# Statistics of the layer norm one tile ahead, key finals between the norms, transposes behind products, and the memory evacuated by VectorE, in a fused linear-attention and gated-MLP kernel

## The chip, the cores and the metric

The kernel runs on one core of a Trainium2 chip. The metric is the device time of one execution in microseconds (us). A run also has a state, fast or slow, told by its granted TensorE clock and its time, and only fast runs are compared. The engines are PE (TensorE, the matrix products), PEld (its weight loads, which overlap products), DVE (VectorE), ACT (ScalarE), POOL (GpSimd) and SP (SyncE, which here only issues DMA). The kernel keeps one queue of DMA on SP and one on ACT.

## The reference

With `x` of 2048 tokens by 640:

```python
xn = layernorm(x)                              # no weights
q, k, v = split(xn @ wqkv)                     # 32 heads of 20
phi = lambda t: where(t > 0, t + 1, exp(t)) + 1e-6
kv  = einsum("bhsd,bhse->bhde", phi(k), v)     # the "memory", over all tokens
o   = einsum("bhqd,bhde->bhqe", phi(q), kv) / (phi(q) . sum_s phi(k) + 1e-6)
g   = silu(relu(xn @ w1) @ w2)
out = x + (o @ wo) * g
```

## The kernel before

The tokens are 16 tiles of 128. The parts that matter here:

- **First keys.** For tiles 0 to 3 there is no time to wait for a full layer norm. The kernel subtracts the mean only (mean on ACT, `mean_act`; subtraction on DVE, `centre`), transposes the tile on PE, copies the transpose to SBUF (`xcT_copy`), multiplies by the key weights (`K_mm`), and applies the reciprocal root later, as a scale of the evacuation (`K_exp`, `K_relu` on ACT, which read `rsy`).
- **Norms.** From tile 4 on there is a true norm on DVE (`LN_norm`). Its statistics are `bn`, `bn`, `aggr` on DVE, and the reciprocal root takes two POOL instructions inside `aggr`. The normed tile is transposed by a DMA that SP issues.
- **Key finals.** `K_fin` finishes phi(k) on DVE in two instructions. Key buffers `ek` are a ring of four, so the evacuation of tile 4 may not start before the final of tile 0.
- **Up products.** `H_block` multiplies by `w1`, which arrives in three parts: 640 KB and 480 KB on SP's queue, 1040 KB on ACT's queue.
- **Memory.** `G_block` is `xn^T phi(k)`, 160 products of 320 columns, evacuated five times.

```python
    def aggr(t):
        sc.op("DVE", lambda eng: eng.bn_aggr(mv[:, t, :], stats[:, t, :, :].rearrange("p a b -> p (a b)")),
              R=[("stats", t, 0), ("stats", t, 1)], W=[("mv", t)])
        sc.op("POOL", lambda eng: eng.tensor_scalar(out=rsv[:, t:t + 1], in0=mv[:, t, 1:2], scalar1=EPS_LN,
                                                    scalar2=None, op0=ALU.add), R=[("mv", t)], W=[("rsv", t)])
        sc.op("POOL", lambda eng: eng.tensor_tensor(out=rsy[:, t:t + 1], in0=rsv[:, t:t + 1], in1=mhalf[:, :],
                                                    op=ALU.pow), R=[("rsv", t), ("mhalf",)], W=[("rsy", t)])

    def LN_stats(t):
        bn(t, 0)
        bn(t, 1)
        aggr(t)

    # ... cut ...

    def LN_norm(t):
        last_norm[0] = sc.op("DVE", lambda eng: eng.tensor_scalar(
            out=xn[:, t, :], in0=xin[:, t % XR, :], scalar1=mv[:, t, 0:1], scalar2=rsy[:, t:t + 1],
            op0=ALU.subtract, op1=ALU.mult), R=[("xin", t % XR), ("mv", t), ("rsy", t)], W=[("xn", t)])
        if t >= 4:
            xnT_dma(t)
        if t + XR < T:
            x_load(t + XR)
```

The first keys as emitted (each engine keeps the order of its own instructions in this text; waits are put in from the data):

```python
    for k in range(KA, C):
        K_mm(0, 2, k, k + 1)
        K_mm(1, 4, k, k + 1)
    bn(1, 1)
    centre(2)
    aggr(1)
    transposes(2, 0)
    mean_act(3, 0)
    bn(2, 0)
    xcT_copy(2, 0, 0, "DVE")
    xcT_copy(2, 0, 1, "DVE")
    K_exp(0, 2)
    K_mm(2, 6, 0, KA)
    K_mm(2, 6, KA, C, (0,))
    centre(3)
    transposes(3, 0)
    K_mm(2, 6, KA, C, (1,))
    bn(2, 1)
    xcT_copy(3, 0, 0, "DVE")
    xcT_copy(3, 0, 1, "ACT")
    w1_load(2, "ACT")
    K_relu(0, 2)
    aggr(2)
    K_mm(3, 0)
    K_exp(1, 4)
    K_relu(1, 4)
    LN_stats(4)
    bn(3, 0)
    bn(3, 1)
    aggr(3)
    K_exp(2, 6)
    K_relu(2, 6)
    K_exp(3, 0)
    K_relu(3, 0)
```

What goes between the up products of the first 512 tokens (`n` is the number of the up block):

```python
            if j == 0:
                if n < 4:
                    LN_norm(n + 4)
                    if n < 3:
                        LN_stats(n + 5)
                if n in (3, 4):
                    K_fin(2 * n - 6)
                    K_fin(2 * n - 5)
                if 4 <= n < 8:
                    LN_norm(n - 4)
                if 8 <= n < 12:
                    xnT_dma(n - 8)
                if n == 8:
                    w_load(wqk[:, :, 0:D], A_wqkv[:, 0:D], ("wq",), E="ACT")
```

The evacuation in `G_block`:

```python
        sc.op("ACT", lambda eng: eng.activation(out=GT[:, k, :].rearrange("p (a n) -> p a n", a=2), in_=ps2(b, HN),
                                                func=ACTF.Copy), R=[("ps", b), ("ps", b + 1)], W=[("GT", k)])
```

## Time and profile before

| | before |
|---|---|
| time, median of 3 runs | 224.86 us (224.37 to 224.89) |
| span of the profiled execution | 223.4 us |
| PE busy | 216.8 us, 97% |
| first up product starts | 12.75 us |
| keys of tile 5 start | 24.48 us |
| the 160 memory products, first start to last end | 22.15 us |

The page of the kernel before: busy time by engine, and the shares of the chain that ended last.

```profile
PE 216.8 (97%) x1442; PEld 133.8 (60%) x1442; DVE 115.0 (51%) x213; ACT 86.6 (39%) x142; POOL 45.9 (21%) x69
...
PE 83%; DVE 4%; ACTq 3%; DMA 3%; SPq 2%; ACT 1%; POOL 1%; issue 1%; DVEq 0%
```

PE is nearly always at work, so the share says little about what a change can win. The Trainium skill (Perfetto Trace Analysis, "Identifying the Most-Contended Engine") warns against TensorE's busy share as a measure of how close a kernel is to its limit. What helps is the list of holes. The timeline of PE early on (columns: start, length, engine, line, instruction, count, and in brackets the idle time just before and what ended it):

```profile
8.73 0.44 PE L470 MATMUL psT<-ident,reg 128*128 128x128 bf16 x5
9.39 1.12 PE L495 MATMUL psT<-reg,regX 128*128 128x320 bf16 x7 [0.22 <-DVE regX L480]
10.35 0.44 PE L470 MATMUL psT<-ident,reg 128*128 128x128 bf16 x5
...
11.38 1.53 PE L495 MATMUL psT<-reg,regX 128*128 128x320 bf16 x10 [0.17 <-ACT regX L482]
12.75 6.64 PE L570 MATMUL psT<-regX,reg 128*128 128x512 bf16 x30
19.22 1.52 PE L495 MATMUL psT<-reg 128*128 128x320 bf16 x10
20.58 2.32 PE L570 MATMUL psT<-regX,reg 128*128 128x512 bf16 x10
24.48 1.53 PE L495 MATMUL psT<-reg 128*128 128x320 bf16 x10 [1.58 <-ACT regE L512]
```

L470 are the transposes, L495 key products and L570 up products. Ten key products take 1.36 us from start to start, and five up products 1.08. This agrees with the Trainium skill (VectorE: DVE Perf Modes, "The TRN2 errata", TensorE row of its table): 6 plus the columns, in cycles of 2.4 GHz, is 136 ns for 320 columns and 216 ns for 512. The large hole is the 1.58 us before the keys of tile 5. The waits of the first 25 us show where it comes from (engine and line, waited for whom: total us, times, longest):

```profile
ACT regE L512 <- DVE reg L530: 3.1, 1, 3.1
DVE reg L435 <- POOL rsy L424: 3.0, 3, 1.0
...
PE psT L495 <- ACT regE L512: 1.6, 1, 1.6
```

PE waits for ACT (L512, the evacuation of tile 4), which waits 3.1 us for a key final on DVE (L530), which is behind norms (L435) that each wait 1.0 us for POOL's root.

The stretch of the memory, all engines (ACTq is ACT issuing DMA):

```profile
112.33 22.15 PE L788 MATMUL psT<-reg 128*128 128x320 bf16 x160
...
114.76 5.70 ACTq L780 DMA_DIRECT2D reg<-in_B_w_dram  x2
120.51 1.42 ACT L793 ACTIVATE reg<-psT 128x640 bf16<-128x640 f32 x2 [7.38 <-issue]
```

ACT issues weight loads until 120.46 us and only then evacuates the first memory block. 64 products of 0.1357 us after 112.33 us, at 121.02, PE would start the third block. It starts at about 121.27, 0.25 us late.

Issues of DMA (size, median us from issue to landing): the two parts of the up weights on SP's queue.

```profile
reg<-in_B_w_dram SPq DMA_DIRECT2D x1, 640.0 KB, 6.7
...
reg<-in_B_w_dram SPq DMA_DIRECT2D x1, 480.0 KB, 7.2
```

They are issued at 5.04 and 6.77 us and land at 11.7 and 14.0.

### The profile page before, as it was taken

Reading aid. Unit: us, or ns where it says so; the run is one execution under the profiler, and the core shown is the slowest. Engines: PE = TensorE matmul, PEld = TensorE weight load, DVE = VectorE, ACT = ScalarE, POOL = GpSimd, SP = SyncE. Lnnn points to the kernel's source line nnn. Section 1 sums busy time; section 2 is a strip of 40 time slices with the busy share of each in tenths; the row PEclk is TensorE's granted clock in tenths of the full one; section 3 lists DMA queues with packets and bytes.
Section 4 is the critical chain, followed back from the end, with each engine's and each line's share of the span. In section 5 each row is a group of like instructions: output and inputs, shape, how many; then the busy total and the mean of one; then the engine's idle time right before and its main releaser. Section 6 shows DMA issues by size and latency. Waiting matters only on the chain.

```text
span 223.4 us, 3512 instructions
## 1 busy us (share of the span) xinstructions
PE 216.8 (97%) x1442; PEld 133.8 (60%) x1442; DVE 115.0 (51%) x213; ACT 86.6 (39%) x142; POOL 45.9 (21%) x69
## 2 busy tenths in 40 slices
PE   8999799999999999999999999999999999999993
PEld 8655354555544555444466777677767776776672
DVE  4766996798649999783700002940424240412243
ACT  4585766656665576554412113232021102110211
POOL 2252631111041599950000005000000000000000
PEclk9999999999999999999999999999999999999999
DMA  6996389621001233000099969900010100001011
GB/s 178 283 339 130 87 248 140 190 44 29 3 1 29 59 94 115 0 0 3 11 204 321 341 245 369 323 12 3 29 59 32 59 29 32 29 29 59 3 59 60
DMA packets 27761, 23.91 MB, mean 107 GB/s; under 512 B 11873, under 2 KB 27105, under 8 KB 27745
## 3 DMA queue, kind: packets, MB, share of 16 engines
q1 hardware_dynamic: 24512, 19.50, 30.7%
q10 hardware_dynamic: 3232, 4.18, 5.4%
q8 instruction: 11, 0.18, 0.3%
q14 instruction: 6, 0.04, 0.1%
HBM read 15.81 MB, written 5.24 MB: 94 GB/s over the span
## 4 chain that ended last, share of the span: by engine, by line
PE 83%; DVE 4%; ACTq 3%; DMA 3%; SPq 2%; ACT 1%; POOL 1%; issue 1%; DVEq 0%
PE psT L840 25%; PE psT L570 21%; PE psT L548 10%; PE psT L879 9%; PE psT L495 7%; PE psT L788 6%; DMA reg<-in_A_x_dram 3%; ACTq L780 3%; DVE stats L416 2%; PE psT L817 1%; PE psT L858 1%; PE psT L587 1%; SPq L358 1%; ACTq L776 1%; POOL rsy L424 1%
## 5 line engine op out<-in xcount | busy, mean ns | idle before, releaser
L840 PE MATMUL psT<-reg,hT 128*128 128x320 bf16 x416 | 60.5, 299 | 0.0
L840 PEld LDWEIGHTS psT<-reg,hT 128*128 128x128 bf16 x416 | 40.3, 98 | 16.5 <-issue 1.1
L570 PE MATMUL psT<-reg 128*128 128x512 bf16 x195 | 46.0, 379 | 0.0
L893 DVE TENSOR_TENSOR reg<-psT,reg 128x640 bf16<-128x640 f32 (+1 forms) x17 | 13.3, 785 | 48.8 <-PE psT L879 47.6
L574 ACT ACTIVATE hT<-psT 128x512 bf16<-128x512 f32 x52 | 30.5, 601 | 17.4 <-PE psT L570 17.4
L570 PEld LDWEIGHTS psT<-reg 128*128 128x128 bf16 x195 | 18.9, 98 | 22.0 <-issue 0.4
L868 ACT ACTIVATE reg<-psT 128x640 bf16<-128x640 f32 x12 | 8.2, 702 | 43.1 <-PE psT L840 23.6
L548 PE MATMUL psT<-reg 128*128 128x512 bf16 x100 | 24.8, 379 | 0.0
L506 POOL TENSOR_TENSOR zacc<-zacc,reg 128x640 f32<-128x640 f32 x16 | 23.8, 1489 | 3.7 <-DVE reg L530 2.8
L879 PE MATMUL psT<-reg,pqT 128*128 128x320 bf16 x160 | 24.3, 299 | 0.0
L788 PE MATMUL psT<-reg 128*128 128x320 bf16 x160 | 22.1, 299 | 0.1
L512 ACT ACTIVATE regE<-psT 128x640 bf16<-128x640 f32 x24 | 15.6, 701 | 11.4 <-PE psT L495 8.3
L495 PE MATMUL psT<-reg 128*128 128x320 bf16 x120 | 18.3, 299 | 1.6 <-ACT regE L512 1.6
L788 PEld LDWEIGHTS psT<-reg 128*128 128x128 bf16 x160 | 15.6, 98 | 6.6 <-ACT reg L793 0.4
L879 PEld LDWEIGHTS psT<-reg,pqT 128*128 128x128 bf16 x160 | 15.7, 98 | 6.1
L556 DVE TENSOR_SCALAR regE<-psT 128x512 bf16<-128x512 f32 x20 | 13.6, 682 | 8.2 <-ACT regE L555 8.2
L558 DVE SCALAR_TENSOR_TENSOR pqT<-regE 128x512 bf16<-128x512 bf16 x20 | 17.4, 870 | 0.7
L548 PEld LDWEIGHTS psT<-reg 128*128 128x128 bf16 x100 | 9.8, 98 | 11.5
L495 PEld LDWEIGHTS psT<-reg 128*128 128x128 bf16 x120 | 11.7, 98 | 8.3 <-ACT regE L512 2.1
L416 DVE BATCH_NORM_STATS2 stats<-reg 128x6 f32<-128x320 bf16 x32 | 14.1, 479 | 3.3 <-DMA reg<-in_A_x_dram 3.3
L806 DVE TENSOR_TENSOR reg<-psT,mv 128x120 bf16<-128x120 f32 (+1 forms) x6 | 1.1, 261 | 27.9 <-POOL reg L910 27.9
L530 DVE TENSOR_TENSOR reg<-regE 128x640 bf16<-128x640 bf16 x16 | 14.5, 909 | 1.4 <-ACT regE L512 1.0
(68 smaller groups left out, 166.6 us busy)
## 6 DMA issues: line engine op xcount, KB each, us to landing
reg<-in_A_x_dram SPq DMA_DIRECT2D x16, 160.0 KB, 3.0
scr<-regE SPq DMA_DIRECT2D x4, 640.0 KB, 11.2
reg<-in_A_x_dram SPq DMA_DIRECT2D x4, 640.0 KB, 9.2
out_dram<-reg SPq DMA_DIRECT2D x15, 160.0 KB, 1.8
regE<-scr SPq DMA_DIRECT2D x4, 512.0 KB, 5.3
reg<-in_B_w_dram ACTq DMA_DIRECT2D x1, 1120.0 KB, 12.3
reg<-in_B_w_dram ACTq DMA_DIRECT2D x1, 1040.0 KB, 6.6
reg<-in_A_wo_dram SPq DMA_DIRECT2D x6, 160.0 KB, 4.2
```

What stands on the lines that cost most here:

```text
L416: sc.op("DVE", lambda eng: eng.bn_stats(stats[:, t, a, :], xv[:, HN * a:HN * (a + 1)]), R=[("xin", t % XR)], W=[("stats", t, a)])
L495: fns.append(lambda eng, a=a, k=k, lhs=lhs: eng.matmul(ps[b + a][:, 0:HN], lhsT=lhs[:, k, tok(t)], rhs=wqk[:, k, D + HN * a:D + HN * (a + 1)],
L506: sc.op("POOL", lambda eng: eng.tensor_tensor(out=zacc[:, :], in0=zacc[:, :], in1=pk[:, t, :], op=ALU.add), R=[("zacc",), ("pk", t)], W=[( ...
L512: sc.op("ACT", lambda eng: eng.activation(out=o_.rearrange("p (a n) -> p a n", a=2), in_=ps2(b, HN), func=func, scale=scale), R=[("ps", b) ...
L530: sc.op("DVE", lambda eng: eng.tensor_tensor(out=pk[:, t, :], in0=e_, in1=r_, op=ALU.add), R=[("ek_e", es), ("ek_r", es)], W=[("pk", t)])
L548: sc.group("PE", [(lambda eng, k=k: eng.matmul(ps[b], lhsT=wqk[:, k, P * f:P * (f + 1)], rhs=xnT[:, k, schunk(j)], start=(k == 0), stop=(k ...
L558: sc.op("DVE", lambda eng: eng.scalar_tensor_tensor(out=pqT[:, f, schunk(j)], in0=e_, scalar=1.0, in1=r_, op0=ALU.min, op1=ALU.add), R=[(" ...
L570: a = sc.group("PE", [(lambda eng, k=k: eng.matmul(ps[b], lhsT=w1_sb[:, k, P * f:P * (f + 1)], rhs=src[:, k, :], start=(k == 0), stop=(k = ...
L574: sc.op("ACT", lambda eng: eng.activation(out=hT[:, f, schunk(j)], in_=ps[b], func=ACTF.Relu), R=[("ps", b)], W=[("hT", j, f)])
L788: fns.append(lambda eng, t=t, a=a: eng.matmul(ps[b + a][:, 0:HN], lhsT=xn[:, t, P * k:P * (k + 1)], rhs=pk[:, t, HN * a:HN * (a + 1)], sta ...
L840: sc.group("PE", [(lambda eng, f=f: eng.matmul(ps[b][:, 0:HN], lhsT=hT[:, f, tok(t)], rhs=w2_sb[:, f, HN * n:HN * (n + 1)], start=(f == 0 ...
L879: sc.group("PE", [(lambda eng, c=c, a=a: eng.matmul(ps[b + a][:, 0:HN], lhsT=pqT[:, c, tok(t)], rhs=wf[:, c, HN * a:HN * (a + 1)], start=( ...
```

## The change

The intent: (1) transpose tile 2 ahead of four products that are ready anyway, so that the copies run behind them; split the products of tile 3 so that the first wait for half of the copy only; do all statistics of tile 3 before those of tile 4. (2) Make the statistics of the next tile before the norm of this one, so that POOL's root is ready, and spread the key finals between the norms. (3) Evacuate the memory on DVE, which is idle there. The third part of the up weights also moves ahead, because on ACT there is no longer a copy in front of it.

```diff
--- before.py
+++ after.py
@@ -613,36 +613,38 @@
     xcT_copy(0, 0, 1, "DVE")
     aggr(0)
     bn(1, 0)
-    for k in range(KA, C):
-        K_mm(0, 2, k, k + 1)
-        K_mm(1, 4, k, k + 1)
     bn(1, 1)
     centre(2)
     aggr(1)
-    transposes(2, 0)
+    bn(2, 0)
     mean_act(3, 0)
-    bn(2, 0)
-    xcT_copy(2, 0, 0, "DVE")
-    xcT_copy(2, 0, 1, "DVE")
+    for k in range(KA, C):
+        if k == C - 1:
+            transposes(2, 0)
+            xcT_copy(2, 0, 0, "DVE")
+            xcT_copy(2, 0, 1, "DVE")
+        K_mm(0, 2, k, k + 1)
+        K_mm(1, 4, k, k + 1)
     K_exp(0, 2)
     K_mm(2, 6, 0, KA)
     K_mm(2, 6, KA, C, (0,))
     centre(3)
     transposes(3, 0)
     K_mm(2, 6, KA, C, (1,))
+    xcT_copy(3, 0, 0, "DVE")
+    xcT_copy(3, 0, 1, "DVE")
     bn(2, 1)
-    xcT_copy(3, 0, 0, "DVE")
-    xcT_copy(3, 0, 1, "ACT")
     w1_load(2, "ACT")
     K_relu(0, 2)
     aggr(2)
-    K_mm(3, 0)
+    K_mm(3, 0, 0, KA)
+    K_mm(3, 0, KA, C)
     K_exp(1, 4)
     K_relu(1, 4)
-    LN_stats(4)
     bn(3, 0)
     bn(3, 1)
     aggr(3)
+    LN_stats(4)
     K_exp(2, 6)
     K_relu(2, 6)
     K_exp(3, 0)
@@ -728,12 +730,11 @@
                 LN_stats(lnat[j][n])
             if j == 0:
                 if n < 4:
-                    LN_norm(n + 4)
                     if n < 3:
                         LN_stats(n + 5)
-                if n in (3, 4):
-                    K_fin(2 * n - 6)
-                    K_fin(2 * n - 5)
+                    LN_norm(n + 4)
+                if 1 <= n < 5:
+                    K_fin(n - 1)
                 if 4 <= n < 8:
                     LN_norm(n - 4)
                 if 8 <= n < 12:
@@ -790,8 +791,8 @@
                     start=(t == 0), stop=(t == T - 1)))
         ag = sc.group("PE", fns, R=[("xn", t) for t in range(T)] + [("pk", t) for t in range(T)],
                       W=[("ps", b), ("ps", b + 1)])
-        sc.op("ACT", lambda eng: eng.activation(out=GT[:, k, :].rearrange("p (a n) -> p a n", a=2), in_=ps2(b, HN),
-                                                func=ACTF.Copy), R=[("ps", b), ("ps", b + 1)], W=[("GT", k)])
+        sc.op("DVE", lambda eng: eng.tensor_copy(GT[:, k, :].rearrange("p (a n) -> p a n", a=2), ps2(b, HN)),
+              R=[("ps", b), ("ps", b + 1)], W=[("GT", k)])
         return ag
 
     def kv_block(c, b):
```

## The prediction

> **What bounds the kernel now.** The busy table gives PE 216.8 us of a 223.4 us span (97%), and the chain of waits is 83% PE. From 24.5 to 218 us the timeline shows PE back to back (ten 320-column products in 1.36 us, five 512-column ones in 1.08). Only holes in PE can pay:
>
> 1. 8.6 to 12.7 us, first keys (timeline): PE waits for the VectorE copy of tile 2's transposes (weight load 0.39 us idle), later for the ScalarE copy of tile 3 (0.51 us).
> 2. 22.9 to 24.48 us (waits view): keys of tile 5 wait 1.58 us for ScalarE, whose evacuation of tile 4 waited 3.1 us for the first key final. That sits behind the norms of tiles 4 to 7, and VectorE idles 1.00 us before three of those, waiting for POOL's reciprocal root of the statistics just made.
> 3. About 121 us: the third block of the memory waits for ScalarE (weight load 0.42 us idle), which issued four weight loads from 112.5 to 120.5 us before evacuating block 0. The 160 products take 21.95 us where 160 x 0.1357 = 21.71 would do: 0.25 us lost.
>
> **What the change does.** No arithmetic is added. Statistics go one tile ahead, so the root (0.22 + 0.57 us on POOL and two hand-offs) runs under the next statistics (1.1 us): the 1.0 us idles vanish. Key final 0 (0.32 + 0.49 us) then ends near 17.6 us instead of 23.0, ScalarE can evacuate tile 4 at once, and hole 2 closes: -1.58 us. Tile 2's transposes move ahead of four ready products (0.54 us), which hide the copy: -0.4 us. Tile 3's first products need only the first copied part: -0.2 us. The memory evacuation costs 0.82 us on VectorE (as in later copies) against 0.70 on ScalarE, but VectorE idles from 110 to 137.9 us: hole 3 closes, -0.25 us.
>
> **What comes back.** (a) ScalarE issues the third part of the up weights about 1.6 us earlier (9.2 instead of 10.84), into DMA at its ceiling (about 375 GB/s from 10.8 to 15.4 us). The Trainium skill (DMA: Bandwidth & Descriptors, "Queues, rings and completion order") says that DMA engines alternate between queues by packets; no trace yet shows how much that delays the first part, which lands at 11.74 us and which PE will want at about 12.1. (b) The transpose of tile 4 is issued near 15.3 us and lands 2.6 to 3.3 us later; PE wants it at 18.6. Estimated loss of (a) and (b): 0.2 us, perhaps 0.7. (c) POOL's accumulations start earlier and stretch VectorE's adds from 0.49 to 1.6 us, as now; not critical.
>
> **Sum.** -1.58 - 0.6 - 0.25 - 0.2 (smaller stalls of the first keys) + 0.2 = -2.4 us. Predicted **222.4 us**, range **221.6 to 223.5**. Faster by over 2% 0.03; within 2% 0.95; slower 0.02.
>
> **What would show it.** Keys of tile 5 start near 22.1 us without waiting for ScalarE; the first up product starts near 12.1 us; VectorE's waits for the root in the first 25 us fall from 3.0 us to near 0; the 160 memory products take 21.7 us; span about 221.
>
> **What would make it wrong.** The first up product waiting for weights until 12.7 us, the keys of tile 4 waiting for their transpose, or a new wait where the memory's last evacuation meets POOL's clearing (134.5 to 137.8 us), which gates the masked values, due before 139.3 us.

## The result, and the profile after

The median went from 224.88 us (4 runs) to 223.26 us (4 runs, 223.05 to 223.55). The ratio is 0.9933, with a 95% interval of 0.9912 to 0.9954. Ratios here are the mean time of one kernel's fast runs over that of the other's in the same rounds, so they are not quite the ratio of the medians quoted. The result lies inside the predicted range, but the gain is 1.6 us where 2.4 was forecast.

| | before | after |
|---|---|---|
| span of the profiled execution | 223.4 us | 221.7 us |
| PE busy | 216.8 us, 97% | 215.7 us, 97% |
| first up product | 12.75 us | about 12.31 us (its own record is missing; worked out below) |
| keys of tile 5 | 24.48 us | 22.30 us |
| keys of tile 8 | 41.51 us | 40.07 us |
| the 160 memory products | 22.15 us | 21.90 us |

The page of the kernel after:

```profile
PE 215.7 (97%) x1432; PEld 133.6 (60%) x1442; DVE 119.5 (54%) x219; ACT 82.8 (37%) x136; POOL 46.9 (21%) x69
...
PE 95%; DVE 1%; DMA 1%; ACT 1%; issue 1%; DVEq 0%
```

PE's busy share is 97% again. In the chain that ended last PE now holds 95% instead of 83: most of the detours over DVE, POOL and DMA, and over ACT's issues, are gone. (Ten records of products are missing from this trace, hence the 215.7. One of them is the first up product: the record at 12.52 is its second. In eleven of the thirteen other profiles the keys of tile 4 start 6.47 or 6.48 us after the first up product; here they start at 18.78, so it started at about 12.31.) PE's timeline after:

```profile
7.92 0.44 PE L470 MATMUL psT<-ident,reg 128*128 128x128 bf16 x5
8.20 1.66 PE L495 MATMUL psT<-reg,regX 128*128 128x320 bf16 x11
9.85 0.45 PE L470 MATMUL psT<-ident,reg 128*128 128x128 bf16 x5
...
12.52 6.42 PE L570 MATMUL psT<-regX,reg 128*128 128x512 bf16 x29 [0.20 <-issue]
18.78 1.52 PE L495 MATMUL psT<-reg 128*128 128x320 bf16 x10
20.14 2.32 PE L570 MATMUL psT<-regX,reg 128*128 128x512 bf16 x10
22.30 1.52 PE L495 MATMUL psT<-reg 128*128 128x320 bf16 x10
```

The tile 2 transposes (7.92) are followed by eleven products without a wait, and the keys of tile 5 start without one. The waits of the first 25 us:

```profile
DVE stats L416 <- DMA reg<-in_A_x_dram: 4.7, 3, 2.3
...
DVE reg L435 <- POOL rsy L424: 0.5, 1, 0.5
```

DVE's wait for the root fell from 3.0 to 0.5 us, and no ACT wait for a key final is left. But DVE waits 4.7 us for inputs now (3.3 before). The two SP loads of up weights in the kernel after:

```profile
reg<-in_B_w_dram SPq DMA_DIRECT2D x1, 640.0 KB, 7.1
...
reg<-in_B_w_dram SPq DMA_DIRECT2D x1, 480.0 KB, 9.9
```

Issued at 5.04 and 6.56, they land at 12.1 and 16.5 us: 0.4 and 2.5 us later than in the profile before. The input of tile 6, behind them, lands at 17.4, not 14.5. The memory stretch:

```profile
110.89 21.90 PE L789 MATMUL psT<-reg 128*128 128x320 bf16 x160
```

The hole of 0.25 us is gone. A new one appears at the keys of tile 8. The chain of the kernel after, there:

```profile
37.39 2.64 DMA reg<-reg
...
40.07 1.53 PE psT L495 x10
```

The DMA is the transpose of normed tile 8. Its norm ends at 36.53 us, but SP has been issuing the transposes of tiles 0 to 3 since 31.58 without a pause and reaches that of tile 8 only at 37.39. From the keys of tile 5 to those of tile 8 takes 17.03 us before and 17.77 after: 0.74 us lost.

So after the first result there were these theories for the missing 0.8 us:

- **A.** The third weight load, issued at 8.68 instead of 10.84 us, takes DMA from the loads ahead of it.
- **B.** SP's queue order delays the transpose of tile 8.
- Rivals: chance in the landings, or products and copies as such.

### The profile page after: what moved, and what is told of

Same layout as the page of the kernel before. It is cut to its first block, busy times and chain, and to the rows that moved or that the text cites. A ratio compares the mean times of both kernels' runs of the same rounds, so it can differ in the third digit from the quotient of the medians.

```text
span 221.7 us, 3502 instructions
## 1 busy us (share of the span) xinstructions
PE 215.7 (97%) x1432; PEld 133.6 (60%) x1442; DVE 119.5 (54%) x219; ACT 82.8 (37%) x136; POOL 46.9 (21%) x69
## 4 chain that ended last, share of the span: by engine, by line
PE 95%; DVE 1%; DMA 1%; ACT 1%; issue 1%; DVEq 0%
PE psT L841 26%; PE psT L570 24%; PE psT L789 10%; PE psT L495 10%; PE psT L880 9%; PE psT L548 9%; PE psT L387 2%; PE psT L818 1%; DMA reg<-reg 1%; PE psT L859 1%; PE psT L587 1%; PE psT L470 1%; PE psT L804 1%; PE psT L676 1%; DVE reg L894 0%
## 5 line engine op out<-in xcount | busy, mean ns | idle before, releaser
L841 PEld LDWEIGHTS psT<-reg,hT 128*128 128x128 bf16 x416 | 40.3, 98 | 16.5 <-issue 1.1
L570 PE MATMUL psT<-reg 128*128 128x512 bf16 x192 | 45.5, 379 | 0.3 <-issue 0.2
L574 ACT ACTIVATE hT<-psT 128x512 bf16<-128x512 f32 x52 | 30.9, 600 | 18.9 <-PE psT L570 18.7
L548 PE MATMUL psT<-reg 128*128 128x512 bf16 x95 | 23.8, 379 | 0.3
L556 DVE TENSOR_SCALAR regE<-psT 128x512 bf16<-128x512 f32 x20 | 13.6, 682 | 8.4 <-ACT regE L555 8.4
L558 DVE SCALAR_TENSOR_TENSOR pqT<-regE 128x512 bf16<-128x512 bf16 x20 | 17.4, 869 | 0.7
L869 ACT ACTIVATE reg<-psT,rsy 128x640 bf16<-128x640 f32 x4 | 3.2, 794 | 37.7 <-PE psT L859 32.5
L794 DVE CAST reg<-psT 128x640 bf16<-128x640 f32 x5 | 4.1, 824 | 20.9 <-PE psT L789 20.9
## 6 DMA issues: line engine op xcount, KB each, us to landing
scr<-regE SPq DMA_DIRECT2D x4, 640.0 KB, 11.3
```

What stands on the lines that cost most here:

```text
L548: sc.group("PE", [(lambda eng, k=k: eng.matmul(ps[b], lhsT=wqk[:, k, P * f:P * (f + 1)], rhs=xnT[:, k, schunk(j)], start=(k == 0), stop=(k ...
L556: sc.op("DVE", lambda eng: eng.tensor_scalar(out=r_, in0=ps[b], scalar1=0.0, scalar2=1e-6, op0=ALU.max, op1=ALU.add), R=[("ps", b), ("er_e ...
L558: sc.op("DVE", lambda eng: eng.scalar_tensor_tensor(out=pqT[:, f, schunk(j)], in0=e_, scalar=1.0, in1=r_, op0=ALU.min, op1=ALU.add), R=[(" ...
L570: a = sc.group("PE", [(lambda eng, k=k: eng.matmul(ps[b], lhsT=w1_sb[:, k, P * f:P * (f + 1)], rhs=src[:, k, :], start=(k == 0), stop=(k = ...
L574: sc.op("ACT", lambda eng: eng.activation(out=hT[:, f, schunk(j)], in_=ps[b], func=ACTF.Relu), R=[("ps", b)], W=[("hT", j, f)])
L841: sc.group("PE", [(lambda eng, f=f: eng.matmul(ps[b][:, 0:HN], lhsT=hT[:, f, tok(t)], rhs=w2_sb[:, f, HN * n:HN * (n + 1)], start=(f == 0 ...
```

## The experiments

Twelve runs were made, in three calls, each on its own chip; before ran beside each call. (One of the twelve is the changed kernel unedited.) All results were correct. "Before beside" had medians of 224.96, 225.15 and 225.12 us.

### Round 1: undo one suspect at a time

**e1_late_load**: the third load back behind the loads it may disturb.

```diff
     xcT_copy(3, 0, 1, "DVE")
     bn(2, 1)
-    w1_load(2, "ACT")
     K_relu(0, 2)
 # ... cut ...
     K_exp(2, 6)
+    w1_load(2, "ACT")
     K_relu(2, 6)
```

> The changed kernel, but the third part of the up weights is issued after the exponential of tile 2 (near 12.4 us) instead of after that of tile 0 (8.68 us). Theory A, the early load takes DMA from the loads ahead of it: the first part lands again near 11.7 us (12.1 in the changed kernel), the second near 14 (16.5), the input of tile 6 near 14.5 (17.4); VectorE's wait of 2.25 us for that input goes; the first up product starts at 12.1 to 12.2 us (12.52) and the 0.24 us hole before the fifth up block goes. Since VectorE then runs about 2 us ahead, the norm of tile 3 and the queue of transposes behind it come earlier too, and the 0.6 us wait of the keys of tile 8 shrinks to under 0.2. Whole time 0.5 to 0.9 us below the changed kernel (ratio to before 0.989 to 0.991). Rival, the early holes come from the products and copies and not from the loads: first up product stays at 12.5, time unchanged (0.993).

Measured: 223.84 us median (222.48 to 224.00), ratio 0.9936 (0.9904 to 0.9968). The landings moved as theory A said: second part 14.2 us, input of tile 6 14.5, and the keys of tile 8 lost nothing (17.02 us after those of tile 5). But the time did not improve, and the first up product started at **13.33** us, later than in the changed kernel. PE waited 0.78 us at the transposes of tile 3:

```profile
11.02 0.45 PE L470 MATMUL psT<-ident,reg 128*128 128x128 bf16 x5 [0.78 <-DVE reg L461]
...
13.33 6.64 PE L570 MATMUL psT<-regX,reg 128*128 128x512 bf16 x30
```

DVE had not yet centred tile 3, since its mean on ACT started at 9.72 us and not at 8.55: the input of tile 3 had landed late, in a load that the edit does not touch. That was in neither theory.

**e2_queue_order**: transposes of tiles 0 to 3 behind that of tile 8.

```diff
-                if 8 <= n < 12:
-                    xnT_dma(n - 8)
 # ... cut ...
             if j > 0 and n - 1 in lnat[j]:
                 LN_norm(lnat[j][n - 1])
+            if j == 1 and 2 <= n < 6:
+                xnT_dma(n - 2)
```

> The changed kernel, but SyncE issues the DMA transposes of normed tiles 0 to 3 after that of tile 8 instead of before it (they are needed only near 45 us). Theory B, the keys of tile 8 wait 0.6 us because their transpose is held in SyncE's queue behind those four (1.2 to 1.6 us each, 31.58 to 37.4 us) although the norm was done at 36.5: the transpose of tile 8 is issued within 0.1 us of the norm's end, the keys of tile 8 start near 39.4 us without a PE wait (40.07 with 0.6 us in the changed kernel), and the whole is 0.6 to 0.75 us shorter (ratio to before 0.990). The early part up to the keys of tile 5 (22.30 us) does not move. Rival, the wait comes from the norm itself being late (POOL's accumulations, VectorE's backlog): keys of tile 8 still wait and the ratio stays 0.993.

Measured: 225.05 us (224.74 to 225.43), ratio 1.0004. The expectation missed. The transpose of tile 8 was indeed issued at 37.38, right after its norm, but the four put behind it came too late for the first query products of tiles 0 to 3, which PE reaches at about 46 us:

```profile
44.74 1.24 PE L570 MATMUL psT<-reg 128*128 128x512 bf16 x5
47.47 1.25 PE L548 MATMUL psT<-reg 128*128 128x512 bf16 x5 [1.49 <-DMA reg<-reg]
```

I had judged that they had time, without working out what stands ahead of them in the queue: issues of about 1.2 us each, a weight load at 39.95 and the transpose of tile 9, whose norm ends at 41.6 us. The wait of 1.5 us is one that the edit made. And the run says nothing about theory B, since other runs with the old order show no wait at tile 8 either (below).

**e3_memory_on_scalar**: only the evacuation back on ACT.

```diff
-        sc.op("DVE", lambda eng: eng.tensor_copy(GT[:, k, :].rearrange("p (a n) -> p a n", a=2), ps2(b, HN)),
+        sc.op("ACT", lambda eng: eng.activation(out=GT[:, k, :].rearrange("p (a n) -> p a n", a=2), in_=ps2(b, HN),
+                                                func=ACTF.Copy),
```

> The changed kernel with only the memory evacuation put back on ScalarE. If that move is worth what the prediction said, the 160 memory products take 21.95 us again (21.73 without a hole) with one weight load waiting 0.4 us for ScalarE, everything before is as in the changed kernel (keys of tile 5 at 22.3), and the whole is 0.25 us longer (ratio to before 0.9945). Rival, ScalarE is not what the third block waits for: no hole, 0.993.

Measured: 223.31 us (222.54 to 223.75), ratio 0.9932: the same as with the move. The timeline of that stretch:

```profile
109.94 21.90 PE L789 MATMUL psT<-reg 128*128 128x320 bf16 x160
...
112.38 5.37 ACTq L781 DMA_DIRECT2D reg<-in_B_w_dram  x2
117.80 0.70 ACT L794 ACTIVATE reg<-psT 128x640 bf16<-128x640 f32 x1 [7.07 <-issue]
```

ACT ended its issues 7.81 us after the first memory product, where it took 8.13 us before. With the evacuation of 0.70 us it is just in time, and there is no hole. The rival was right for this run.

**e4_both**: e1 and e2 together.

```diff
-    w1_load(2, "ACT")
     K_relu(0, 2)
 # ... cut: w1_load(2, "ACT") after K_exp(2, 6), as in e1 ...
-                if 8 <= n < 12:
-                    xnT_dma(n - 8)
 # ... cut: xnT_dma(n - 2) at j == 1, 2 <= n < 6, as in e2 ...
```

> Late third weight load and the transposes of tiles 0 to 3 after that of tile 8, together. If theories A and B both hold and the late load already frees most of the queue, this is little better than the better of the two alone: 0.7 to 1.0 us below the changed kernel, ratio to before 0.9885 to 0.990, keys of tile 5 at 22.1 us, those of tile 8 near 39.2 without a wait. If the two losses are independent it is the sum of both gains.

Measured: 224.80 us (224.52 to 225.09), ratio 0.9992. It missed for the reason of e2 (a wait of 1.8 us at the same query products). Its early part is as good as any: first up product at 12.10 us, with the mean of tile 3 at 8.44.

**After round 1** the profiles pointed at something else. In e1 to e4 the first up product starts 3.61, 3.60, 3.61 and 3.66 us after the mean of tile 3 starts, and that start is the landing of its input (ACT waits for it). It varies: 8.44 to 9.72 us, though no edit touches the loads before it. This became **theory D: the change moves PE's early limit from the holes to the landing of the input of tile 3**, which the kernel before did not feel. The start of that mean on ACT, in the kernel before and in e1:

```profile
8.30 0.74 ACT L450 ACTIVATE regE<-reg 128x640 bf16<-128x640 bf16 x1 [1.13 <-DMA reg<-in_A_x_dram]
...
9.72 0.74 ACT L450 ACTIVATE regE<-reg 128x640 bf16<-128x640 bf16 x1 [2.55 <-DMA reg<-in_A_x_dram]
```

### Round 2: one part of the change alone, and a kernel that takes the landing off the path

**p1_order_only**: before with the second hunk only (statistics ahead, finals between).

```diff
                 if n < 4:
-                    LN_norm(n + 4)
                     if n < 3:
                         LN_stats(n + 5)
-                if n in (3, 4):
-                    K_fin(2 * n - 6)
-                    K_fin(2 * n - 5)
+                    LN_norm(n + 4)
+                if 1 <= n < 5:
+                    K_fin(n - 1)
```

> The kernel before with only the second part of the change: statistics one tile ahead of the norms, key finals between them. Theory C, the 1.58 us hole before the keys of tile 5 hung on the first key final alone: the hole is gone, VectorE's three 1.0 us waits for the root are gone or under 0.5 in all, the first up product stays near 12.75 us and the keys of tile 5 start near 22.7 to 22.9 instead of 24.48. Ratio to before 0.9925 to 0.994 (-1.4 to -1.7 us). Rival, most of the gain comes from the first keys: ratio above 0.996.

Measured: 223.89 us (223.11 to 224.39), ratio 0.9945 (0.9918 to 0.9972), a gain of 1.2 us. Keys of tile 5 at 22.79 without a wait; DVE's waits for the root 0.5 us in all; first up product at 12.80. Theory C holds in the trace; the ratio lies just outside the expected 0.9925 to 0.994, and its interval alone would not rule out the rival. This part makes most of the gain.

**p2_first_keys_only**: before with the first hunk only.

```diff
+    for k in range(KA, C):
+        if k == C - 1:
+            transposes(2, 0)
 # ... cut: the whole first hunk of the change ...
-    LN_stats(4)
     bn(3, 0)
     bn(3, 1)
     aggr(3)
+    LN_stats(4)
```

> The kernel before with only the first part of the change (transposes behind products, copies of tile 3 on VectorE, statistics of tile 3 before those of tile 4, third weight load earlier). The first up product starts 0.3 to 0.6 us earlier when the input of tile 3 lands near 8.5 us, and later than 12.75 when it lands after 9.2 (3.6 us after it, by four runs of the changed kernel's order). But the keys of tile 5 still wait for ScalarE and through it for the norms, a chain that starts at the input of tile 4 (12.24 us before): they start at 24.3 to 24.9 us whatever the first keys do, so the time is that of before, ratio 0.998 to 1.003. Prediction's own sum would give 0.996 to 0.997 for this part (-0.6 to -0.8 us).

Measured: 226.47 us, ratio 1.0071 (1.0033 to 1.0109). It was **slower**, which neither I nor the prediction had expected. Two of its six runs had a granted clock of 0.99; the other four have a mean of 226.12 us, against 225.06 for the fast runs of before beside it, so about 1.1 us is the kernel's own. In its profile, DVE:

```profile
10.58 0.39 DVE L461 TENSOR_SCALAR reg<-reg,msum 128x640 bf16<-128x640 bf16 x1 [1.18 <-ACT regE L450]
...
12.46 0.83 DVE L416 BATCH_NORM_STATS2 stats<-reg 128x6 f32<-128x320 bf16 x2
...
13.45 0.83 DVE L416 BATCH_NORM_STATS2 stats<-reg 128x6 f32<-128x320 bf16 x2
...
15.53 0.45 DVE L435 TENSOR_SCALAR reg<-reg,mv,rsy 128x640 bf16<-128x640 bf16 x1 [0.99 <-POOL rsy L424]
```

The norm chain, which without the second hunk still leads to the keys of tile 5, now stands behind tile 3: centred at 10.58 (its mean started at 9.72), its statistics at 12.46, and only then those of tile 4 at 13.45, where they were at 12.24 before. The keys of tile 5 start at 25.62 us, 1.14 us later than before. In the kernel before, DVE did the statistics of tile 4 first and those of tile 3 behind.

**p3_memory_only**: before with the third hunk only.

```diff
-        sc.op("ACT", lambda eng: eng.activation(out=GT[:, k, :].rearrange("p (a n) -> p a n", a=2), in_=ps2(b, HN),
-                                                func=ACTF.Copy), R=[("ps", b), ("ps", b + 1)], W=[("GT", k)])
+        sc.op("DVE", lambda eng: eng.tensor_copy(GT[:, k, :].rearrange("p (a n) -> p a n", a=2), ps2(b, HN)),
+              R=[("ps", b), ("ps", b + 1)], W=[("GT", k)])
```

> The kernel before with only the memory evacuation on VectorE. Prediction: the 160 products take 21.73 us instead of 21.95, -0.25 us, ratio 0.9989. Rival from the run with the memory back on ScalarE, where no hole was seen because ScalarE's four load issues ended 7.86 us after the first memory product and not 8.18: the hole comes and goes with the issue time of the weight loads, so the mean gain is under 0.2 us and may not be told from zero (0.9985 to 1.0005). The early part repeats that of before: keys of tile 5 at 24.3 to 24.8 us.

Measured: 224.96 us (223.83 to 225.58), ratio 0.9991 (0.9957 to 1.0026). The products took 21.90 us with no hole, but the time can't be told from that of before. With the evacuation on ACT, PE started the third block late by 0.25 (before), 0.51 (p1), 0.35 (p2), 0.22 (h2 below), 0 (e3) and 0 us (p4 below): 0.22 us on average, worked out from the starts of the blocks in each timeline as above. The delay follows the time that ACT's last two load issues took: 5.25 and 5.37 us where it was 0 (p4, e3), then 5.66, 5.70, 5.79 and 5.96 us (h2, before, p2, p1).

**g1_input3_first**: the changed kernel with the input of tile 3 loaded earlier, and the products that need the last row of key weights put later.

```diff
-    for k in range(KA, C):
-        wk_load(k)
-    x_load(3)
+    wk_load(KA)
+    x_load(3)
+    for k in range(KA + 1, C):
+        wk_load(k)
 # ... cut ...
-    for k in range(KA, C):
-        if k == C - 1:
+    for k in range(KA, C - 1):
+        if k == C - 2:
             transposes(2, 0)
 # ... cut ...
-    K_exp(0, 2)
     K_mm(2, 6, 0, KA)
-    K_mm(2, 6, KA, C, (0,))
+    K_mm(2, 6, KA, C - 1)
     centre(3)
     transposes(3, 0)
-    K_mm(2, 6, KA, C, (1,))
+    K_mm(0, 2, C - 1, C)
+    K_mm(1, 4, C - 1, C)
+    K_mm(2, 6, C - 1, C)
+    K_exp(0, 2)
 # ... and the third weight load after K_exp(2, 6), as in e1
```

> The changed kernel with the input of tile 3 loaded ahead of the fourth and fifth rows of key weights, the last row's products of tiles 0, 1 and 2 put behind the transposes of tile 3, and the third part of the up weights issued after the exponential of tile 2. Theory D, the changed kernel's first up product starts 3.6 us after the input of tile 3 lands, and that landing varies from 8.4 to 9.7 us from run to run: here that input lands near 7.5 us and has 1 us to spare, the first up product starts at 12.0 to 12.4 us in every run, the rest takes 208.7 us, and the time is 222.3 to 222.7 with little spread: ratio 0.989 to 0.9905, about 0.8 us below the changed kernel. Rival, the spread lies elsewhere (weights of the up product, ScalarE): ratio stays 0.993.

Measured: 222.61 us (222.29 to 224.17), ratio 0.9904 (0.9871 to 0.9937), the best ratio of all kernels. Its mean of tile 3 started at 7.19 us. In a2 below the transposes start 1.30 us after that mean; here they start at 9.69, so the landing has about 1.2 us to spare:

```profile
9.69 0.44 PE L471 MATMUL psT<-ident,reg 128*128 128x128 bf16 x5
...
12.29 6.64 PE L571 MATMUL psT<-regX,reg 128*128 128x512 bf16 x30
```

Not all went as expected: one run took 224.17 us, so the spread did not vanish. The changed kernel did not run in this call, and the two intervals overlap, so that g1 beats the changed kernel is likely but not shown. It also holds two edits at once (landing and late load).

### Round 3: doses

**a2_changed_again**: the changed kernel unedited.

> The changed kernel again, unedited, for a second profile and for its time beside the others on this chip. Expected ratio 0.9925 to 0.994; first up product 3.6 us after the mean of tile 3 starts unless the first part of the up weights lands later; input of tile 6 after 15.5 us; a wait of the keys of tile 8 of 0 to 0.8 us, the larger the later that input.

Measured: 223.19 us (222.95 to 224.34), ratio 0.9914 (0.9856 to 0.9972). The runs of before beside it include one of 227.13 us at a clock of 0.992; without it the mean of before is 225.11, that of a2 is 223.42, and the ratio 0.9925, close to the 0.9933 of the first measurement. The input of tile 6 was expected after 15.5 and landed at about 14.9 us. The chain of this profile shows theory D from end to end (start, length, what):

```profile
4.56 4.61 DMA reg<-in_A_x_dram
...
9.83 0.20 ACT regE L450
...
10.05 0.40 DVE reg L461
...
10.49 0.30 PE psT L470 x2
...
10.81 0.57 DVE regX L480 x2
...
11.43 1.53 PE psT L495 x10
12.96 6.47 PE psT L570 x30
```

Input of tile 3 landing at 9.17, mean (read out at 9.83), centre, transposes, copies, ten products, up products: from the landing on, each piece of the chain starts as the one before it ends, and PE never catches up. The keys of tile 8 lost nothing here. (The line of DMA is followed back by the profile to its issue at 4.56.)

**h1_changed_input3_late** and **h2_before_input3_late**: two inputs loaded ahead of that of tile 3, in the changed kernel and in the kernel before.

```diff
-    x_load(3)
-    w1_load(0, "SP")
     x_load(4)
     x_load(5)
+    x_load(3)
+    w1_load(0, "SP")
```

> The changed kernel with the inputs of tiles 4 and 5 loaded ahead of that of tile 3 (same bytes, tile 3 about 0.9 us later). Theory D, in the changed kernel the first up product follows that landing by 3.6 us and nothing later gives the time back: mean of tile 3 starts near 9.4 us or later, first up product at landing plus 3.6 (13.0 or later, as late as 14 in a run where the landing is late as well), the whole 0.7 to 1.0 us longer than the changed kernel, ratio to before 0.996 to 0.9985. Rival, the landing of tile 3 is not what sets the time: ratio 0.992 to 0.994.

> The same reordering of loads in the kernel before. Theory D, the kernel before does not feel it, because its keys of tile 5 wait for VectorE's chain of norms that starts at the input of tile 4, which now lands earlier: first up product up to 0.5 us later, hole before the keys of tile 5 that much shorter, keys of tile 5 at 24.2 to 24.7 us as before, ratio 0.998 to 1.001. Rival, the input of tile 3 sets the time in both kernels: ratio 1.003 to 1.005.

Measured, h1: 224.07 us (223.83 to 224.41), against 223.19 of the changed kernel. By the means, 224.10 against 223.42, it is 0.7 us longer, which four runs of each don't lift clear of the noise. (The ratio to before, 0.9944, missed the forecast of 0.996 to 0.9985; without the run at the low clock it is 0.9955.) The mean of tile 3 started at 10.23 and PE's up products at 13.84, again 3.61 us later, with 1.82 us of wait at the transposes. The traces are firmer than the times: from the first up product to the end of the span, e3, g1, a2, e1 and h1 take 208.7 to 208.9 us, although that product starts anywhere from 12.11 to 13.84 us. Measured, h2: 225.02 us (224.67 to 225.44), ratio 0.9986 (0.9931 to 1.004), or 0.9997 without the run of before at the low clock. Its first up product came at 13.36, 0.6 us later than before, and yet it lost no time: the input of tile 4 landed earlier, the norm chain started at 11.60, and the hole before the keys of tile 5 shrank to 0.26 us, so that these keys started even earlier than expected (23.77 us, not 24.2 to 24.7):

```profile
13.36 6.64 PE L570 MATMUL psT<-regX,reg 128*128 128x512 bf16 x30
...
23.77 1.53 PE L495 MATMUL psT<-reg 128*128 128x320 bf16 x10 [0.26 <-ACT regE L512]
```

So, by the traces, the kernel before has slack for tile 3 and the changed kernel has none.

**p4_early_load**: before with only the third load moved ahead.

```diff
     K_exp(0, 2)
+    w1_load(2, "ACT")
 # ... cut ...
-    w1_load(2, "ACT")
     K_relu(0, 2)
```

> The kernel before with the third part of the up weights issued right after the exponential of tile 0 (near 8.6 us instead of 10.84). Theory A, the early load delays the loads ahead of it in the other queue: second part of the up weights lands 1 to 2.5 us later than its 13.97 us, input of tile 6 1 to 2.5 us later than 14.45, first part and input of tile 4 0.2 to 0.5 later than 11.74 and 12.2. Here that costs little, since the norm chain reaches tile 6 only at 17.2 us: ratio 0.999 to 1.003. Rival, the late landings seen in the profile of the changed kernel are chance: landings within 0.5 us of those of before.

Measured: 225.13 us (224.36 to 225.38), ratio 0.9979 (0.9913 to 1.0044); without the run of before at the low clock 0.9995. The load was issued at 9.46 us, because ACT sat in its wait for the input of tile 3. The second part of the up weights landed 9.2 us after its issue, at 15.9, and the input of tile 6 at 16.9:

```profile
reg<-in_B_w_dram SPq DMA_DIRECT2D x1, 480.0 KB, 9.2
```

Theory A holds for the landings, and they cost this kernel nothing that can be measured.

### All profiles side by side

Start times in us, read from the timelines. "Mean 3" is the start of tile 3's mean on ACT.

| kernel | order of first keys | mean 3 | first up product | difference | keys of tile 5 | 5 after first up product |
|---|---|---|---|---|---|---|
| before | before | 8.30 | 12.75 | 4.45 | 24.48 | 11.73 |
| p3 | before | 8.22 | 12.45 | 4.23 | 24.02 | 11.57 |
| p4 | before | 9.37 | 13.08 | 3.71 | 24.94 | 11.86 |
| p1 | before | 8.77 | 12.80 | 4.03 | 22.79 | 9.99 |
| h2 | before | 9.65 | 13.36 | 3.71 | 23.77 | 10.41 |
| after | changed | 8.55 | 12.31 (worked out) | 3.76 | 22.30 | 9.99 |
| a2 | changed | 9.19 | 12.80 | 3.61 | 22.79 | 9.99 |
| e1 | changed | 9.72 | 13.33 | 3.61 | 23.32 | 9.99 |
| e2 | changed | 9.52 | 13.12 | 3.60 | 23.12 | 10.00 |
| e3 | changed | 8.50 | 12.11 | 3.61 | 22.10 | 9.99 |
| e4 | changed | 8.44 | 12.10 | 3.66 | 22.19 | 10.09 |
| h1 | changed | 10.23 | 13.84 | 3.61 | 23.84 | 10.00 |
| p2 | changed | 9.72 | 13.33 | 3.61 | 25.62 | 12.29 |

(g1 has an order of its own: 7.19, 12.29, 22.28.) Two readings. The last column falls from 11.6 to 11.9 (12.3 in p2) to 10.0 exactly where the second hunk is in: that is the hole of 1.4 to 1.7 us, and it closes every time. (Of the kernels without that hunk only h2, whose loads were moved, comes near, with 10.4.) The fifth column is 3.6 with the changed first keys (3.8 in after) and 3.7 to 4.5 with the old ones: the changed first keys gain 0.1 us when the input lands late, and 0.4 to 0.8 only when it lands early, as it did in the one profile from which the prediction was made.

## Why the prediction was right or wrong

- **Hole 2, -1.58 us: right in mechanism and size.** By the last column of the table it and its restart were worth 1.6 to 1.9 us. The hole is gone in every profile with the new order of norms and finals (p1, after, a2, e1 to e4, h1, g1). Alone, timed, it is worth 1.2 us (p1), with an interval of 0.6 to 1.8.
- **Hole 3, -0.25 us: right on average, but not a fixed sum.** It was 0 to 0.51 us in six profiles with ACT, 0.22 on average, since it hangs on how long ACT's last two weight loads take to issue (5.3 to 6.0 us). In time it could not be told from zero (p3, e3).
- **First keys, -0.4, -0.2 and -0.2 us, with +0.2 us coming back: right in mechanism, with a size that holds only when the input of tile 3 lands early.** The step that was mis-sized is "Tile 2's transposes move ahead of four ready products (0.54 us), which hide the copy: -0.4 us. Tile 3's first products need only the first copied part: -0.2 us." Both holes do close. But behind them stands the input of tile 3, 3.61 us ahead of the first up product, and it landed at 8.2 to 9.7 us in the eleven profiles that load it in the old order. The forecast was read from a profile in which it landed early (8.30). With inputs nearly as early (8.50 and 8.44), e3 and e4 do start their up products at 12.1 us against 12.75, as forecast; that is luck in the landing. Over the six profiles of after, a2 and e1 to e4 the start is 12.63 us on average, and over before, p1, p3 and p4 12.77. This 0.14 us understates the gain, since the six happened to have later inputs (mean 3 at 8.99 us on average, against 8.67). At equal landings the fifth column gives some 0.3 to 0.5 us, an estimate, where 0.6 net was forecast. In time, e3 (first and second hunk) lies 0.0013 of the ratio below p1 (second hunk alone), or 0.3 us, which is not clear of the noise. The dose runs h1 and h2 show the sensitivity itself.
- **What comes back, (a): the direction was right and the place wrong.** The early load delayed the second part of the weights by up to 2.5 us. For the first part no delay is shown: it landed at 11.2 to 12.2 us with the early load, issued before 10 us, and at 11.3 to 11.9 in the other profiles with the old order on SP's queue. In a2, e1 and e3 the keys of tile 5 start 13.60 us after the mean of tile 3; in the profile of after it is 13.75, so PE lost about 0.15 us at its first up product, whose weights had landed at 12.1 us. That it waited for them is likely and not shown; the waits view names ACT. In the time of p4, or by undoing it in e1, no loss could be told.
- **(b): right.** In after, the transposed tile 4 landed at 18.6 us, as forecast, and PE's weight load waited 0.2 us for it; PE itself lost nothing there.
- **Not foreseen:** the 0.74 us at the keys of tile 8. Of the nine profiles with the new order of norms and finals only that of after shows it; the others have 17.0 us between the keys of tiles 5 and 8. In after the input of tile 6 landed at 17.4 us, the latest of all, DVE's norms of tiles 0 to 3 ended at 30.9 us (28.8 in a2), and SP's transposes started at 31.58 instead of 28.9 to 30.4 (p1, e1, e3, a2, h1, g1). In e3 that input landed at 16.1 and the transposes started at 30.05, still in time. That the late input causes the wait is read from the traces; the run that was to test it (e2) made a wait of its own, so this stays open as a cause.
- **(c): off the critical path, as said.** DVE's adds are stretched from 0.49 to 1.62 us while POOL accumulates. The Trainium skill (GPSIMD Engine Reference, "1. Specifications") says that GpSimd's SBUF interfaces are shared with VectorE; the numbers agree.

The sum, stage by stage, against the profile before. In after: first up product -0.44 us, from there to the keys of tile 5 -1.74, tile 8 +0.74, memory -0.25, together -1.69, where the spans differ by 1.7. In a2 the input of tile 3 landed late and tile 8 lost nothing: +0.05, -1.74, 0 and -0.25, together -1.94, where the spans differ by 1.8. In e3 the input landed early, tile 8 lost nothing, and the memory, though on ACT, had no hole: -0.64, -1.74, 0 and -0.25, together -2.63, where the spans differ by 2.6. That run took 222.54 us, so the forecast of 222.4 can be reached. By these profiles, the 0.8 us that the median lacks are a late input of tile 3 in some runs and the wait at tile 8 in others. How often each comes is not known, since only profiled runs show it. The range held both, but the prediction had named neither.

## What to carry to other kernels

When a hole closes, ask what the work behind it waits for next, and look at how much that moment varies from run to run, because slack read from one profile can be an input that happened to land early. Moving a producer one step ahead of its consumer pays in full when the wait between them is on the chain (1.4 to 1.7 us of hole in the traces here), and reordering that is harmless with it can cost time without it (p2). Before shifting instructions in an in-order queue, count the issues that then stand before each user (e2).

## What the Trainium skill lacked or had wrong

- DMA: Bandwidth & Descriptors ("Latency and other measured facts") gives latencies of HBM with and without load, but not how much one load's landing varies between executions: the same 160 KB load, ninth on its queue, landed 3.6 to 5.1 us after its issue in eleven profiles, and the time of the kernel followed it.
- The same page ("Queues, rings and completion order") says that queues take turns by packets, and the landings agree in direction, but not how much: loads already queued on SP landed up to 2.5 us later in three of the four profiles in which a load of 1040 KB was issued on ACT's queue before 9.5 us (second part at 16.5 us in after, 15.9 in p4 and 15.1 in e3, but 13.8 in a2), and not later than 14.4 when it was issued after that.
- The same page ("Issuing engines are not separate DMA queues") calls the sequencer's time to issue a DMA usually small relative to the DMA itself. On ACT, two loads of 80 KB took 5.3 to 6.0 us to issue behind two large ones (the two landed 13.6 us after issue, median, in the kernel before). There the issues held up ACT's first evacuation of the memory until 120.51 us, by about 3.6 us: DVE, in the kernel after, starts it 4.55 us after the first product, which would be 116.9.
